# A fused forgetting-attention and gated feed-forward kernel on one core: the mask of its first blocks by TensorE, its first loads row by row, and a new order of the queues

## The chip, the cores and the metric

The kernel runs on one core of a Trainium2 chip. The core has five engines that take their own instruction queues in order and meet only at semaphores: TensorE (PE in the profile; its weight loads are PEld), VectorE (DVE), ScalarE (ACT), GpSimd (POOL) and SyncE (SP). SP, POOL and ACT also issue the DMAs, which 16 DMA engines carry out. The metric is device time in microseconds (us) of one execution; lower is better. Most executions of one kernel agree within a few tenths of a per cent, but the three runs shown below spread by 1.7%.

## The reference

```python
def _attn_ref(q, k, v, f):                    # q, k, v: (8, 8, 576, 64), f: (8, 8, 576)
    scores = scale * np.matmul(q, k.transpose(0, 1, 3, 2))
    cum = np.cumsum(np.log(np.clip(f, 0.0001, 1.0)), axis=-1)
    decay = cum[:, :, :, None] - cum[:, :, None, :]
    scores = np.where(causal, -1000000000.0, scores + decay)
    attn = np.exp(scores - np.max(scores, axis=-1, keepdims=True))
    attn = attn / (np.sum(attn, axis=-1, keepdims=True) + 1e-09)
    return np.matmul(attn, v)

def _moe_ref(x, w_gate, w_val, w_out, rms_g):  # x: (4608, 512), hidden width 1536
    xn = x / np.sqrt(np.mean(x * x, axis=-1, keepdims=True) + 1e-06) * rms_g
    g = xn @ w_gate
    return g * (1.0 / (1.0 + np.exp(-g))) * (xn @ w_val) @ w_out
```

Eight batches of eight heads attend causally over 576 positions with a decay by the cumulated log of the forget gate. The heads are then joined to rows of 512, normalised, and sent through a gated feed-forward. All arrays are float32 at the boundary; the kernel's matmuls take bfloat16.

## The kernel before, in words

**Tiles.** A block (b, qi) is 128 query positions of one batch, all eight heads; qi runs from 0 to 3, and qi = 4 (`LAST`) is the remaining 64 positions, which are taken for two batches together. The feed-forward works on groups of 512 rows: four blocks are one group (`home`). The first four batches run as a wave: group 0 is the block qi = 0 of batches 0 to 3, group 1 their qi = 1, and so on. Batches 4 to 7 then run one after the other, and group 8 collects all remainders.

**One block.** q, k are loaded with a cast to bfloat16 (POOL's DMA queue), and turned so that the head dimension lies on partitions: by PE for the first eight blocks (`turn_pe`, a transpose into the buffers `ff` and a copy to QT by DVE and to KT by ACT), by DMA for the others (`turn`, issued by SP). v is loaded in float32 and scaled by the decay factor (`scale_v`, tile Vs; POOL, but DVE for the very first). `score_block` multiplies KT with QT into one of two score buffers `sc`, ACT takes exp into PT, and the diagonal tile is masked: by POOL's affine_select (L596), for the four blocks of group 0 by a minimum with the tile `keep` on DVE (L602). `values` multiplies PT with Vs in two halves (even heads, odd heads), each into an `ff` buffer; an extra column of Vs gives the sum of weights, whose reciprocal scales the copy to x (L637, L639). `norm` forms the mean square (DVE, L667, or ACT, L653), takes its power of -1/2 on POOL (rs, L672), scales x to xn (L679, L683), turns it to xT by PE or DMA, and, for the first two groups, multiplies by rgT, the norm weights as four columns (L699).

**One group.** `gate` makes 12 pairs of products of xT with `wg` and `wv` (L771), tanh on ACT, two multiplications on DVE into hT (L786, L778). `project` multiplies hT with `wo` (L802) for each of four row tiles, ACT copies the result to `ores` (L814), and a DMA stores it (L820, or L828 for group 8). For the first two groups the gate products are cut into 256 rows, so that two blocks are enough to begin.

**First loads.** In wave order q and k of (b, 0), b = 0 to 3, come first, then the weights in four pieces each (`load_w`; c0 to c1 are 256, 256, 512 and 512 columns), then blocks (0, 1), (1, 1) and `wo`. The eight loads of (b, 0) fetch two neighbouring rows with one packet (`paired`), into tiles `T_two` that borrow the space of the rings `ores`, `ga` and `th`; `turn_pe` then needs 16 transposes of 64x64 and a copy with a stride. The four v loads of these blocks and rgT are issued by SP (`load_early`); rgT waits for the first Q copy.

**The order.** Nothing is scheduled by hand. Every piece of work is a `Unit` with an engine, a price in us, a due time (`key`), what it needs and which ring buffers it takes and gives back. `Plan.run` plays the units through in model time: a free engine takes the ready unit with the lowest key whose buffers are free, and the order in which units are taken becomes the order of the queues. The table `SHIFTS` moves the key of each unit, in the order in which the units were made, by so many hundredths. The prices and keys only set the order; the chip keeps to the order and the semaphores.

## Time and profile before

| | |
|---|---|
| three runs | 376.1, 378.63, 382.45 us (median 378.63) |
| the profiled execution | 376.78 us, its span 375.1 us, granted PE clock 0.997 |
| DMA traffic | 152922 packets, 45.05 MB; read from HBM 38.16 MB, written 9.44 MB |
| exp (L588) | 100 instructions of 1022 ns on ACT |
| gate products (L771) | 94.0 us with wg, 94.1 us with wv |
| projection (L802) | 102.2 us |
| scores (L569), values (L622) | 32.4 us, 36.9 us |

The span is the time from the first to the last instruction. The profile gives the busy time of each engine, 40 equal slices of it, the chain of work that ended last, and instructions grouped by line. In a timeline row stand start, length, engine, line, operation, what is written and what is read, and in brackets how long the engine had been idle before and what ended that. Matmuls are pipelined and their ends modelled, so a group's busy time is less than count times mean.

### The profile page before, as it was taken

The page shows a single profiled execution, that of the slowest core. Times are in us where ns is not written, and L with a number is a line of the kernel's source. Part 1 is how long each engine was busy: PE and PEld are TensorE (multiplying, and loading weights), DVE is VectorE, ACT ScalarE, POOL GpSimd, SP SyncE. Part 2 cuts the span into 40 slices and gives each one's busy share as a digit, 9 for nine tenths or more (in the row PEclk, how much of TensorE's full clock was granted, in tenths as well). Part 3 has the DMA queues.
Part 4 walks back from the last instruction along what each step waited for, and adds up shares of the span by engine and source line. Part 5 has one row for each costly group of instructions (what it writes and reads, how often), then busy time and mean ns, then how long its engine had stood idle before and what let it go on. Part 6 is the DMA issues. An engine that isn't in the chain of part 4 may idle for free.

```text
span 375.1 us, 8971 instructions
## 1 busy us (share of the span) xinstructions
PE 351.7 (94%) x3569; PEld 203.7 (54%) x3617; DVE 237.1 (63%) x460; ACT 206.7 (55%) x310; POOL 190.3 (51%) x259
## 2 busy tenths in 40 slices
PE   2669999999999998999999999999999999999995
PEld 2548876677755555545455455445455544444453
DVE  6758776599766857666545667655467782473520
ACT  5544666686677657735675667336777331333122
POOL 8776999999899738843534396424112000000000
PEclk9999999999999999999999999999999999999998
DMA  9999999999999959993958999960602000201024
GB/s 127 178 204 212 207 190 166 196 152 128 161 173 183 156 84 178 179 187 63 192 97 93 165 124 139 182 100 31 136 8 56 2 16 29 82 3 56 18 49 102
DMA packets 152922, 45.05 MB, mean 120 GB/s; under 512 B 141424, under 2 KB 147312, under 8 KB 152880
## 3 DMA queue, kind: packets, MB, share of 16 engines
q0 software_dynamic: 77856, 17.83, 53.9%
q1 hardware_dynamic: 74944, 26.58, 37.0%
q8 instruction: 28, 0.46, 0.5%
q14 instruction: 14, 0.11, 0.1%
q10 hardware_dynamic: 80, 0.07, 0.1%
HBM read 38.16 MB, written 9.44 MB: 127 GB/s over the span
## 4 chain that ended last, share of the span: by engine, by line
PE 85%; DVE 6%; DMA 5%; issue 2%; ACT 1%; POOL 1%; ACTq 0%; DVEq 0%; SPq 0%
PE ff L771 47%; PE ff L802 24%; PE sc L569 7%; PE ff L622 6%; DMA rgT<-in_moe_rms_g_dram 3%; DMA QT<-qk 2%; DVE junk L667 1%; DVE x L639 1%; DVE ga L786 1%; DVE hT L778 1%; DVE Vs L327 1%; DVE xn L683 1%; PE ff L692 0%; POOL rs L672 0%; PE ff L515 0%
## 5 line engine op out<-in xcount | busy, mean ns | idle before, releaser
L588 ACT ACTIVATE PT<-sc 128x1024 bf16<-128x1024 f32 x100 | 99.4, 1022 | 41.2 <-PE sc L569 35.5
L786 DVE SCALAR_TENSOR_TENSOR ga<-th,ff 128x512 f32<-128x512 f32 x108 | 73.6, 685 | 55.2 <-ACT th L784 51.1
L802 PE MATMUL ff<-wo,hT 128*128 128x512 bf16 (+1 forms) x421 | 102.2, 373 | 1.5 <-issue 0.5
L784 ACT ACTIVATE th<-ff 128x512 f32<-128x512 f32 x108 | 64.2, 598 | 64.5 <-PE ff L771 55.5
L771 PE MATMUL ff<-xT,wg 128*128 128x512 bf16 (+1 forms) x465 | 94.0, 340 | 2.5 <-DVE rden L637 0.9
L771 PE MATMUL ff<-xT,wv 128*128 128x512 bf16 (+1 forms) x472 | 94.1, 337 | 0.8 <-DVE hT L778 0.2
L778 DVE SCALAR_TENSOR_TENSOR hT<-ga,ff 128x512 bf16<-128x512 f32 x108 | 72.9, 685 | 26.9 <-PE ff L771 20.5
L771 PEld LDWEIGHTS <-wg 128*128 128x128 bf16 x528 | 50.2, 99 | 41.7 <-issue 2.2
L771 PEld LDWEIGHTS <-wv 128*128 128x128 bf16 x528 | 50.4, 98 | 40.3 <-issue 0.3
L802 PEld LDWEIGHTS <-hT 128*128 128x128 bf16 x444 | 40.5, 98 | 41.2
L596 POOL TENSOR_SCALAR_AFFINE_SELECT PT<-PT 128x1024 bf16<-128x1024 bf16 x32 | 36.2, 1134 | 41.9 <-ACT PT L588 38.7
L540 POOL TENSOR_TENSOR Vs<-v,decT 128x512 bf16<-128x512 f32 (+1 forms) x39 | 41.7, 1069 | 24.7 <-DMA v<-in_v_dram 24.1
L814 ACT COPY ores<-ff 128x512 f32<-128x512 f32 (+1 forms) x37 | 21.1, 572 | 39.5 <-PE ff L802 39.4
L622 PEld LDWEIGHTS <-PT 128*128 128x128 bf16 (+1 forms) x960 | 32.8, 103 | 17.4 <-issue 7.2
L622 PE MATMUL ff<-Vs,PT 128*128 128x65 bf16 (+1 forms) x960 | 36.9, 196 | 4.3 <-POOL Vs L541 3.0
L672 POOL TENSOR_TENSOR rs<-ms,mhalf 128x1 f32<-128x1 f32 (+1 forms) x28 | 17.9, 639 | 38.4 <-ACT junk L653 34.5
L569 PE MATMUL sc<-QT,KT 64*128 64x128 bf16 (+1 forms) x960 | 32.4, 211 | 3.7 <-DVE rgT L321 1.8
L569 PEld LDWEIGHTS <-KT 64*128 64x128 bf16 x960 | 24.0, 95 | 18.1 <-issue 14.3
L639 DVE TENSOR_TENSOR x<-ff,rden 128x256 f32<-128x256 f32 x72 | 30.6, 424 | 2.5
L398 POOL DMA_DIRECT2D qk<-in_q_dram x36 | 31.3, 873 | 0.6 <-issue 0.5
L398 POOL DMA_DIRECT2D qk<-in_k_dram x36 | 31.3, 872 | 0.3 <-DMA wo<-in_moe_w_out_dram 0.3
L683 DVE SCALAR_TENSOR_TENSOR xn<-x,rs,rgB 128x512 bf16<-128x512 f32 x28 | 24.4, 898 | 10.6 <-POOL rs L672 10.6
(67 smaller groups left out, 165.0 us busy)
## 6 DMA issues: line engine op xcount, KB each, us to landing
out_dram<-ores SPq DMA_DIRECT2D x32, 256.0 KB, 2.4
v<-in_v_dram SPq DMA_DIRECT2D x20, 256.0 KB, 5.4
qk<-in_k_dram POOLq DMA_DIRECT2D x28, 128.0 KB, 5.6
qk<-in_q_dram POOLq DMA_DIRECT2D x28, 128.0 KB, 6.2
v<-in_v_dram POOLq DMA_DIRECT2D x12, 256.0 KB, 6.9
wo<-in_moe_w_out_dram POOLq DMA_DIRECT2D x2, 768.0 KB, 11.4
wg<-in_moe_w_gate_dram POOLq DMA_DIRECT2D x2, 512.0 KB, 11.9
wv<-in_moe_w_val_dram POOLq DMA_DIRECT2D x2, 512.0 KB, 13.7
```

Source lines behind the costliest of these rows:

```text
L398: nc.gpsimd.dma_start(out=T_qk[h.slot][0:n, :].rearrange("p (h d) -> p h d", d=D), in_=src[b, :, p0:p0 + n, :].rearrange("h p d -> p h d"))
L540: eng.tensor_tensor(T_Vs[hv.slot][0:n, j, :, 0:D], T_v32[h.slot][0:n, :, :], bcast(dj, D), ALU.mult)
L569: nc.tensor.matmul(t[:, par, c:c + n], lhsT=kt[r, p, kj * 128:(kj + 1) * 128], rhs=qt[r, p, qi * 128:qi * 128 + n], start=True, stop=True)
L588: nc.scalar.activation(T_PT[hp.slot].rearrange("p (a c) -> p a c", a=2), T_sc[h.slot], ACT.Exp, scale=scale)
L596: nc.gpsimd.affine_select(out=d, in_=d, pattern=[[0, 1024 // n], [1, n]], compare_op=ALU.is_ge, fill=0.0, base=0, channel_multiplier=-1)
L622: nc.tensor.matmul(po[i * n:(i + 1) * n, p, :], lhsT=T_PT[h.slot][:, c:c + n], rhs=T_Vs[hold_Vs[x].slot][:, kj, 2 * p + par, :], start=(kj ...
L639: nc.vector.tensor_tensor(d, po[:, :, 0:D], bcast(rden[par], D), ALU.mult)
L771: nc.tensor.matmul(T_ff[h.slot][:, c:c + n], lhsT=w[:, dc, fc * 128:(fc + 1) * 128], rhs=xT[:, dc, t0:t0 + n], start=(dc == 0), stop=(dc = ...
L778: nc.vector.scalar_tensor_tensor(hT, in0=three[0], scalar=0.5, in1=three[1], op0=ALU.mult, op1=ALU.mult)
L784: th = act(0.6, key - 0.1, lambda: nc.scalar.activation(T_th[ht.slot], T_ff[hg.slot], ACT.Tanh, scale=0.5), [ug], take=[ht])
L786: a = dve(0.72, key - 0.1, lambda: nc.vector.scalar_tensor_tensor(T_ga[ha.slot], in0=T_th[ht.slot], scalar=1.0, in1=T_ff[hg.slot], op0=ALU ...
L802: nc.tensor.matmul(T_ff[hf.slot][:, 0:nc0], lhsT=T_hT[hold_hT[g].slot][:, fc, j * 128:(j + 1) * 128], rhs=wo[:, fc, cols], start=(fc == 0) ...
```

## The change

Seven things change in the code beside the table of the order.

1. *Mask.* For the four blocks of group 0, DVE's minimum goes. `keep` holds 0 on and above the diagonal and -1e30 below, and a new PE unit `bias` multiplies the identity with it into both halves of the score buffer, ahead of the scores; these then accumulate onto it (`start` is False) and exp makes zeros of the masked places. The unit has its own key, 0.6 before that of the scores.
2. *Loads.* `paired`, `T_two` and the ring `two` go; q and k of (b, 0) are loaded like all others, row by row into the ring `qk`, with four transposes of 128x128 and a plain copy.
3. *Values of the last 64* come as one PE unit that takes both `ff` buffers at once, not two units.
4. *The last product* (group 8, row tile 3) is cut into 384 and 128 columns instead of two times 256; the first piece is three units, the second one unit that waits for all of hT; the copy of the second piece is made by DVE. The products of group 8 end in the order of their row tiles (`ends`).
5. *Engines.* Vs of blocks (1, 0) and (2, 0) is scaled by DVE instead of POOL; the mean squares of blocks (0, 0) and (1, 0) are taken by ACT instead of DVE.
6. *Constants.* The fills of `mhalf` and of the extra column of x become a unit of their own on POOL.
7. *Prices* of many units, among them the loads, transposes and the model's factor for two moving queues.

The table SHIFTS is replaced as a whole; its entries were between -176 and 179 hundredths and are now between -1096 and 758. For the first queues its first row says, with the keys in the code, that POOL issues q before k of block (0, 0), and the mask tile after the first five of the eight loads.

```diff
-    -1, 1, 1, -1, 31, 0, -20, 14, -46, 25, -13, -12, -5, -46, 48, -19, 3, 10, 12, 42, -64, 71, 12, -62, 39, -70,
+    0, 0, 0, 0, -361, 0, -195, 96, 11, 156, -197, -432, -88, 210, -192, -173, 83, 80, -41, -101, -109, -86, 90, -63,
...
-        nc.gpsimd.memset(keep, 3.0e38)
-        nc.gpsimd.affine_select(out=keep, in_=keep, pattern=[[1, 128]], compare_op=ALU.is_ge, fill=0.0, base=0,
+        nc.gpsimd.memset(keep, 0.0)
+        nc.gpsimd.affine_select(out=keep, in_=keep, pattern=[[1, 128]], compare_op=ALU.is_ge, fill=-1.0e30, base=0,
...
-    iden_f = pool(0.95, -29.5, emit_ident)
-    keeps = pool(1.4, -28.5, emit_keep)
+    iden_f = pool(0.58, -29.5, emit_ident)
+    consts = pool(0.38, -28.45, emit_const)
+    keeps = pool(0.65, -28.5, emit_keep)
...
-            h = hold_qk[b, nm, j] = Hold("two" if paired(b, j) else "qk", 1)
-            if paired(b, j):
-                def emit(src=src, h=h):
-                    nc.gpsimd.dma_start(out=T_two[h.slot],
-                                        in_=src[b, :, 0:128, :].rearrange("h (p r) d -> p h r d", r=2))
...
+            h = hold_qk[b, nm, j] = Hold("qk", 1)
...
-        add, dur, eng = (dve, 0.8, nc.vector) if early else (pool, 1.5, nc.gpsimd)
+        add, dur, eng = (dve, 0.8, nc.vector) if early or (j == 0 and b in (1, 2, -1)) else (pool, 1.6 if j == 0 and b < WAVE else 1.25, nc.gpsimd)
...
                             nc.tensor.matmul(t[:, par, c:c + n], lhsT=kt[r, p, kj * 128:(kj + 1) * 128],
-                                             rhs=qt[r, p, qi * 128:qi * 128 + n], start=True, stop=True)
-        deps = pads if last_block[0] is None else [last_block[0]]
+                                             rhs=qt[r, p, qi * 128:qi * 128 + n], start=(b, qi) not in FAST,
+                                             stop=(b, qi) not in FAST or p == 3)
+        deps = list(pads) if last_block[0] is None else [last_block[0]]
         gives = []
+        if tiles[0][:2] in FAST:
+            h0 = holds[0]
+
+            def bias():
+                m = bass.AP(tensor=keep.tensor, offset=keep.offset, ap=[keep.ap[0], [0, 4], [1, 128]])
+                for par in range(2):
+                    nc.tensor.matmul(T_sc[h0.slot][:, par, :], lhsT=ident, rhs=m, start=True, stop=False)
+            u = pe(0.86, key - 0.6, bias, [iden, keeps] + ([last_bias[0]] if last_bias[0] else []), take=[h0])
+            last_bias[0] = u
+            deps.append(u)
...
-            if items[-1][1] == qi:
+            if items[-1][1] == qi and (b, qi) not in FAST:
...
-                if (b, qi) in FAST:
-                    def mk(hp=hp):
-                        d = T_PT[hp.slot].rearrange("p (h q) -> p h q", q=128)
-                        m = bass.AP(tensor=keep.tensor, offset=keep.offset, ap=[keep.ap[0], [0, 8], [1, 128]])
-                        nc.vector.tensor_tensor(d, d, m, ALU.min)
-                    masked[b, qi].append(dve(0.65, key, mk, [e, keeps]))
-                else:
-                    masked[b, qi].append(pool(1.1, key, mk, [e]))
+                masked[b, qi].append(pool(1.1, key, mk, [e]))
...
+        hpos = [Hold("ff", 1) for _ in range(2)]
+        units = []
+        for pars in ((0, 1),) if qi == LAST else ((0,), (1,)):
...
-        if b < WAVE and js[0] < LAST and len(js) == 1 and (js[0] or b in (0, 1)):
+        if b < WAVE and js[0] < LAST and len(js) == 1 and (js[0] or b in ()):
...
-            hf, cols = Hold("ff", 1), slice(x * nc0, (x + 1) * nc0)
+            hf, cols = Hold("ff", 1), slice(x * 384, 384 + x * 128) if halves == 2 else slice(0, DM)
+            wide = cols.stop - cols.start
+            parts = 3 - 2 * x
...
+            add, copy = (dve, nc.vector.tensor_copy) if x else (act, nc.scalar.copy)
...
+        if g == B:
+            ends.append(last)
```

More of the change, by code (lines that the diff above doesn't have):

```diff
@@ L578, in score_block @@
         cols = sum(len(items) * n / 128 for b, qi, items, n in tiles)
[L579 to L580 removed]
+        u = pe(0.19 + 0.25 * cols, key, emit, deps, take=holds, give=gives)
         last_block[0] = u
```

129 lines of the change are left out of this document (56 added, 73 removed), and 142 rows, old and new, of the table SHIFTS.

## The prediction

> **What bounds the kernel now.** I read the page first: its engine shares, its slices and the chain that ended last.
>
> ```profile
> span 375.1 us, 8971 instructions
> ...
> PE 351.7 (94%) x3569; PEld 203.7 (54%) x3617; DVE 237.1 (63%) x460; ACT 206.7 (55%) x310; POOL 190.3 (51%) x259
> ...
> PE   2669999999999998999999999999999999999995
> ...
> DMA  9999999999999959993958999960602000201024
> ...
> PE 85%; DVE 6%; DMA 5%; issue 2%; ACT 1%; POOL 1%; ACTq 0%; DVEq 0%; SPq 0%
> ```
>
> TensorE (PE) is busy for 351.7 of 375.1 us, and the chain that ended last lies on it for 85%. The slices say where the other 23.4 us are: PE shows 2 and 6 tenths in the first 19 us, 9 almost everywhere after that, and 5 in the last slice. The DMA row is at 9 for the first third of the span. So there are two questions: when does the dense PE work begin, and what holds the beginning up? The busy time by stage, cut where the first gate product starts and where the last product ends, gives the sizes:
>
> ```profile
> 0.00:24.07 24.07, 10.86 (x206) 9.19 (x207) 17.45 (x50) 12.95 (x17) 19.15 (x41) 1.00 1.29 163
> 24.07:370.85 346.78, 340.85 (x3364) 194.54 (x3411) 219.66 (x411) 193.21 (x293) 171.19 (x219) 1.00 0.90 117
> 370.85:375.10 4.25, 0.00 (x0) 0.00 (x0) 0.00 (x0) 0.59 (x1) 0.00 (x0) 0.77 0.30 93
> ```
>
> Columns: stretch and length, then PE, its weight loads, DVE, ACT and POOL busy. PE idles 24.07 - 10.86 = 13.21 us before the first gate product, 346.78 - 340.85 = 5.93 us in the stream, and 4.25 us at the end. Three terms follow: start, stream, tail. The chain of waits, in order of time, and the timeline of the start come next:
>
> ```profile
> 9.16 12.37 DMA rgT<-in_moe_rms_g_dram
> ...
> 24.07 3.57 PE ff L771 x16
> ...
> 30.28 4.37 PE ff L771 x40
> ```
>
> ```profile
> 9.16 3.89 SPq L453 DMA_DIRECT2D rgT<-in_moe_rms_g_dram  x1
> ...
> 9.65 0.69 DVE L602 TENSOR_TENSOR PT<-PT,keep 128x1024 bf16<-128x1024 bf16 x1
> ...
> 12.36 1.02 ACT L588 ACTIVATE PT<-sc 128x1024 bf16<-128x1024 f32 x1 [2.03 <-PE sc L569]
> ...
> 14.06 0.68 DVE L602 TENSOR_TENSOR PT<-PT,keep 128x1024 bf16<-128x1024 bf16 x1
> ...
> 15.97 0.40 PE L622 MATMUL ff<-Vs,PT 128*128 128x65 bf16 x4
> ...
> 17.05 0.73 DVE L522 COPY QT<-ff 128x512 bf16<-128x512 bf16 x1
> ...
> 18.48 0.42 DVE L639 TENSOR_TENSOR x<-ff,rden 128x256 f32<-128x256 f32 x1
> ...
> 20.16 1.04 POOL L540 TENSOR_TENSOR Vs<-v,decT 128x512 bf16<-128x512 f32 x1 [1.96 <-DMA v<-in_v_dram]
> ...
> 21.30 0.56 POOL L672 TENSOR_TENSOR rs<-ms,mhalf 128x1 f32<-128x1 f32 x1
> ...
> 21.56 0.69 DVE L699 TENSOR_TENSOR xT<-ff,rgT 128x512 bf16<-128x512 bf16 x1 [1.32 <-DMA rgT<-in_moe_rms_g_dram]
> ...
> 23.32 0.69 DVE L699 TENSOR_TENSOR xT<-ff,rgT 128x512 bf16<-128x512 bf16 x1
> ```
>
> The first gate product needs both xT tiles of blocks 0 and 1, and two things hold them. The norm weights rgT are issued at 9.16 and land 12.37 us later, at 21.5; the first xT (L699) waits for them. The second xT, at 23.32, hangs on rs at 21.30, which stood on POOL behind the Vs of 20.16, which waited 1.96 us for a v load. Block 1's own chain was long too: exp ended at 13.38, DVE masked only at 14.06, the values product ran at 15.97. The start is thus set by loads, and by DVE and POOL taking their work in order. Two rows of the chain also give a price for cold PE: 16 products of 256 columns in 3.57 us (223 ns each) at 24.07, but 40 in 4.37 us (109 ns) at 30.28.
>
> **The change part by part.** All is set against this execution's own 376.78 us (span 375.1 and 1.7 around it).
>
> *Mask on PE.* Four DVE masks (L602, 0.68 to 0.69 us each) go; eight matmuls of 128x512 come, two for a block. No row has a cold 512-column matmul; from the 223 ns above it is 2 x 223 = 446 ns, so 0.89 us a block and 3.6 us in all. I cost them at nothing, because PE idles 13.21 us there and the unit has only to wait for the mask tile, the identity and a free score buffer. If that cover is gone (the score buffer still read by exp, or the mask tile late on POOL behind the first loads), PE's queue stands still, the transposes and values behind it too, and 0.89 us each for the two blocks of the first gate is 1.8 us on the path.
>
> *Less on DVE and POOL.* The Vs scaling of blocks 1 and 2 goes from POOL (1.04 us each) to DVE, and the sums of squares of blocks 0 and 1 from DVE to ACT:
>
> ```profile
> L653 ACT ACTIVATE junk<-x 128x513 bf16<-128x513 f32 x2 | 1.3, 628 | 0.8 <-DVE x L639 0.8
> ...
> L667 DVE SCALAR_TENSOR_TENSOR junk<-x 128x513 bf16<-128x513 f32 x2 | 1.4, 698 | 0.1
> ```
>
> Plain instead of strided PSUM copies shorten the four Q copies, as line 524 stands to 522:
>
> ```profile
> L522 DVE COPY QT<-ff 128x512 bf16<-128x512 bf16 x4 | 2.9, 720 | 0.0
> ...
> L524 DVE COPY QT<-ff 128x512 bf16<-128x512 bf16 x4 | 1.7, 421 | 0.4 <-PE ff L515 0.4
> ```
>
> DVE loses 4 x 0.68 + 2 x 0.70 + 4 x 0.30 = 5.3 us and gains two Vs of about 0.69 (the duration of its 512-column rows in the timeline): net 3.9 us of the 17.45 it works before 24.07. For block 1: exp to values falls from 2.59 us (13.38 to 15.97) to about 0.2, saving 2.4; of the Q copy and the next mask that stood before x at 18.48 about 1.0 goes; and rs no longer stands behind the Vs that waits, saving some 1.6 (x done at 18.90, its squares about 0.8 later, rs at 21.30). Alone that brings the second xT 5.0 us forward, to about 18.3. Then rgT is what is late next: two xT of 0.69 us after 21.54 end at 22.9, so the first gate comes at 23.0 if rgT does not move, a gain of 1.1.
>
> *One-row loads.* Eight q and k loads come as 1024 packets instead of 512: 4096 more packets on POOL's queue, and 16 transposes become 4 on an idle PE (nothing). The rate of the two kinds stands in the DMA rows of 3:5 us (two-row packets alone) and of 34:35 us (nearly all one-row packets):
>
> ```profile
> DMA packets 1040, 0.26 MB, mean 129 GB/s; under 512 B 1040, under 2 KB 1040, under 8 KB 1040
> ```
>
> ```profile
> DMA packets 1088, 0.20 MB, mean 200 GB/s; under 512 B 1072, under 2 KB 1072, under 8 KB 1088
> q0 software_dynamic: 1088, 0.20, 228.5%
> ```
>
> 1040 in 2 us is 0.98 us a load of 512; 1072 in 1 us is 0.96 us a load of 1024. Alone, then, the one-row load costs nothing more. If each small packet took the time of a two-row one, a load would take 1.97 us and eight of them 7.9 us more. Bounds: 0 and 7.9. I take 2.0, near the lower end, since the second row has the very packets in question, but not 0, because the early loads share the engines with v. In the Trainium skill, "DMA: Bandwidth & Descriptors" (Why small descriptors are slow) gives a fixed overhead of about 3 cycles a packet beside one cycle for 32 B. By an estimate from that page two packets of 128 B need 14 cycles where one of 256 B needs 11, so 8 x 0.98 x 0.27 = 2.1 us more; the 34:35 row shows no such surplus, and the sum would be the same by it to 0.1 us.
>
> The gate's first weights are behind these packets:
>
> ```profile
> 9.03 1.55 POOL L421 DMA_DIRECT2D wg<-in_moe_w_gate_dram  x2
> ```
>
> ```profile
> wg<-in_moe_w_gate_dram POOLq DMA_DIRECT2D x1, 256.0 KB, 10.5
> ```
>
> They land at 9.03 + 10.5 = 19.5 now and at about 21.5 then. But rgT stands in the other queue, behind the v packets. In 14:18 us the two queues moved packet for packet:
>
> ```profile
> q0 software_dynamic: 982, 0.47, 86.8%
> q1 hardware_dynamic: 977, 0.25, 46.9%
> ```
>
> There a software packet took 0.868 x 64 / 982 us, 57 ns; in 34:35 it is 2.285 x 16 / 1088 us, 34 ns. Opposite one-row packets the 7.5 us that rgT still needs after 14 could shrink towards 34/57 of that, 3 us at most and by my estimate 2; if the start is bound by the number of packets, it comes no sooner than now. The first gate starts then between 21.6 (first weights) and 23.0 (rgT unmoved). I take the middle, 22.3: **start -1.8 us**, bounds -3.5 and +3.4 (weights 7.9 us later, gate at 27.5).
>
> *What is late next.* The following weights and the loads of the next four blocks are 2 us later while PE is 1.8 earlier. From 24 to 54 us PE has hardly any room:
>
> ```profile
> 24.00:54.00 30.00, 29.20 (x315) 24.48 (x316) 22.85 (x48) 17.65 (x30) 25.23 (x32) 1.00 1.54 205
> ```
>
> Only 0.80 us of idle; the four products of the first output group are ready as filler once wo has come. I give back **+0.8 us**, bounds 0 and 3.8 (both shifts in full).
>
> *The order.* The new table of shifts changes the queues of all engines for the whole stream, PE, SP's transposes and POOL's issues among them. The trace cannot show it; what it shows is that 5.93 us of idle are there to win, in pieces no longer than this one:
>
> ```profile
> PE ff L771 <- DVE rden L637: 0.9, 1, 0.9
> ```
>
> Many small waits can be neither all removed nor much improved by one order: I take **-0.5 us**, bounds -4 (two thirds of the idle gone) and +6 (idle doubled). The last-64 values in one piece have the same matmuls; only the first evacuation waits for the second half, hidden while two of four ff buffers are free; without that cover four times about 0.4 us (half of one). Split constants, new prices and the plain buffers change no work.
>
> *The tail.* The last product is cut into 384 and 128 columns instead of twice 256, the same column count, and its last copy is 128 wide, on DVE, then stored by SP and ACT. Before, another row tile ended the kernel:
>
> ```profile
> 371.09 0.59 ACT L814 COPY ores<-ff 128x512 f32<-128x512 f32 x1 [0.70 <-PE ff L802]
> 371.70 0.34 SPq L820 DMA_DIRECT2D out_dram<-ores  x1
> ```
>
> ```profile
> out_dram<-ores SPq DMA_DIRECT2D x1, 256.0 KB, 2.0
> out_dram<-ores SPq DMA_DIRECT2D x3, 64.0 KB, 1.9
> out_dram<-ores ACTq DMA_DIRECT2D x1, 64.0 KB, 2.2
> ```
>
> A copy of 512 columns took 0.59 us. For 128 I take 0.3 (the Q copies' 0.42 is above it): -0.3. The store of 64 rows lands in 1.9 to 2.2 us against 2.0: +0.1. **Tail -0.2 us**, bounds -0.6 and +0.3.
>
> **Sum:** 376.78 - 1.8 + 0.8 - 0.5 - 0.2 = 374.3; the three runs before have a median of 378.63, 1.85 above the profiled one, with a lowest of 376.1. I add 0.7 of this spread, as the new runs will scatter likewise: 375.0.
>
> **The rivals.**
> *A. The loads take over (slower).* Place: POOL's DMA queue from 2 to 30 us. If each one-row packet costs what a two-row one costs, the first weights land at 27.4, the gate starts at 27.5, 3.4 us late, and the next four blocks, 7.9 us late, add another 2 when PE runs out of filler: 376.8 + 5.4 = 382. With s us more for the loads the gate starts at 19.6 + s and the give-back is 0.4 s (0.8 for 2.0); with order and tail at -0.7 the sum s - 4.5 + 0.4 s - 0.7 turns positive at s = 3.7, which is where it decides. For it: the DMA row at 9 and rgT already 12.37 us in flight. Against it: the 1088 packets of 34:35.
> *B. Nothing arrives.* rgT stays at 21.5, the gate starts at 23.0, and the 1.1 us go in the stream before 54 us, where DMA sets the pace: 376.8 - 1.1 + 1.1 - 0.2, with the same 0.7 about 377.3. For it: the 0.80 us of idle there.
> *C. Everything arrives.* rgT early, gate at 21.0 to 21.6, -2.8; the order takes 3 us of the 5.93; tail -0.5: 376.8 - 6.3 = 370.5. For it: block 1 has 5 us to gain and idle that the waits show as avoidable. Against: loads at 9 tenths.
> *D. The mask units block PE's queue* as priced above, +1.8: the start gains nothing, and 376.8 + 0.8 - 0.5 - 0.2 with the 0.7 is 377.6, close to B and counted with it.
>
> **How the numbers follow.** The forecast of 374 to 376.5 has 0.48, C 0.18, B with D 0.22, A 0.12. The predicted time is 375.0. The range goes from C's 370.5 to 381, which leaves out most of A and the better part of what lies under C: about 2 in 10. Two per cent, 7.6 us, is about what a measurement of this kernel can tell from no change. Faster by that means below 371.1, about half of C: 0.10. Slower means above 386.2, beyond A's 382 and reached only with a worse order on top: 0.04. The rest, 0.86, is within.
>
> **What would show it.** Right: no DVE mask in the first 24 us and 128x512 matmuls before the scores; values of block 1 before 14 us; rs of block 1 not behind a waiting Vs; first gate product at 21.6 to 23.0; PE idle in the stream of 5 to 7 us; 4 us from the last product to the end. Wrong: the first gate after 24.1 with the first weights landing late (A); a PE wait before the masks' matmuls (D); idle between 30 and 60 us above 2 us (B); stream idle below 3 us (C) or above 9 (order). The forecast falls if rgT lands after 22, or if the stream's idle is far from 6.

## The result and the profile after

The changed kernel took 382.65 us (median of 12 runs, 379.74 to 389.29), the kernel before 377.75 us beside it (12 runs, 375.57 to 382.45). The ratio is 1.0133, 95% interval 1.0088 to 1.0177: 1.3% longer, clear of the scatter though under two per cent, where 375.0 us (370.5 to 381.0) had been forecast. Ratios leave out runs more than 1.5% above the fastest of the same kernel. The profiled execution took 379.88 us, 3.1 us more than the 376.78 us of the one before. The page of the changed kernel, the rows that answer to those shown of before, with the row of the granted PE clock (first that of before, then that of after):

```profile
span 378.1 us, 8861 instructions
...
PE 357.2 (94%) x3529; PEld 202.3 (53%) x3529; DVE 232.2 (61%) x457; ACT 207.4 (55%) x313; POOL 189.7 (50%) x255
...
PE   3979999999999998899999999999999999999995
...
PE 66%; POOL 14%; DMA 8%; issue 4%; DVE 4%; ACT 2%; SPq 1%; DVEq 0%; POOLq 0%
```

```profile
PEclk9999999999999999999999999999999999999998
```

```profile
PEclk9969999999999999999999999999999999999999
```

PE is as busy as before (94%), and the slices look alike. What differs is the chain that ended last: PE held 85% of it, now 66%, and POOL 14%, DMA 8%; and the clock, which is at 6 tenths in the third slice (18.9 to 28.4 us). The stages, cut again at the first gate product and the last product (columns as above):

```profile
0.00:22.97 22.97, 12.97 (x113) 7.72 (x114) 13.81 (x45) 13.27 (x20) 18.07 (x37) 0.98 1.41 153
22.97:373.56 350.59, 344.27 (x3420) 194.57 (x3417) 218.13 (x411) 194.16 (x294) 171.65 (x219) 0.99 0.91 117
373.56:378.10 4.54, 0.00 (x0) 0.00 (x0) 0.29 (x1) 0.00 (x0) 0.00 (x0) 0.86 0.42 116
```

The start is 1.10 us shorter (22.97 against 24.07), the tail 0.29 us longer (4.54 against 4.25), the stream 3.81 us longer (350.59 against 346.78): together the 3.0 us by which the span grew. The timeline of the start:

```profile
8.90 1.06 PE L571 MATMUL sc<-keep,ident 128*128 128x512 bf16 x2
...
14.58 0.43 PE L617 MATMUL ff<-Vs,PT 128*128 128x65 bf16 x4
...
18.80 1.05 POOL L531 TENSOR_TENSOR Vs<-v,decT 128x512 bf16<-128x512 f32 x1 [2.48 <-DMA v<-in_v_dram]
...
19.94 0.55 POOL L668 TENSOR_TENSOR rs<-ms,mhalf 128x1 f32<-128x1 f32 x1
20.17 0.69 DVE L695 TENSOR_TENSOR xT<-ff,rgT 128x512 bf16<-128x512 bf16 x1 [3.14 <-DMA rgT<-in_moe_rms_g_dram]
...
22.21 0.68 DVE L695 TENSOR_TENSOR xT<-ff,rgT 128x512 bf16<-128x512 bf16 x1
...
22.97 1.26 PE L767 MATMUL ff<-xT,wg 128*128 128x256 bf16 x5
```

The mask's product is made first, and nothing masks on DVE. Block 1's values run at 14.58 us instead of 15.97. rgT lands 1.4 us earlier, the first xT being released at 20.17 instead of 21.56. But the second xT comes only at 22.21: rs of block 1 stands at 19.94, right behind a Vs on POOL that waited 2.48 us for its v load. It is the Vs of block 3, which the change left on POOL.

Then the lead is lost, most of it within seven microseconds. The stretch in which the changed kernel's granted clock is at half (stretch and length, PE's busy time and count, granted clock, DMA share, GB/s):

```profile
21.87:28.69 6.82, 6.03 (x38) 0.50 1.28 205
```

The page of before shows no such stretch, but the first clock entry of its trace comes only at 28.44 us, and its products ran as slowly until then: 16 of them in 3.57 us, as the prediction's chain shows. So both kernels begin the gate at half rate and reach full rate at about the same time. The gate products that follow the first 32, before and after:

```profile
30.12 1.04 PE L771 MATMUL ff<-xT,wg 128*128 128x256 bf16 x8
```

```profile
29.81 1.91 PE L767 MATMUL ff<-xT,wv 128*128 128x256 bf16 x16
```

Of the 1.10 us, 0.31 are left. Gate products done after 44 us (timeline windows of that line alone; PE's busy time and count, then weight loads, clock, DMA share, GB/s), before first, after second:

```profile
0.00:44.00 44.00, 18.19 (x136) 13.90 (x136) 1.00 1.36 184
```

```profile
0.00:44.00 44.00, 18.60 (x136) 14.11 (x136) 0.92 1.42 178
```

Both kernels have done 136. The rest goes mainly at one place. PE waits 4.1 us for xT in the changed kernel, 3.43 of them at once. The stretch around it, first before, then after:

```profile
138.58 0.08 DVE L667 DVE_READ_ACCUMULATOR junk<-x 128x1 f32 x1
...
139.63 0.54 POOL L672 TENSOR_TENSOR rs<-ms,mhalf 128x1 f32<-128x1 f32 x1
...
140.21 0.75 DVE L683 SCALAR_TENSOR_TENSOR xn<-x,rs,rgB 128x512 bf16<-128x512 f32 x1 [0.95 <-POOL rs L672]
...
141.03 1.23 SPq L703 DMA_TRANSPOSE xT<-xn  x1
...
142.98 4.07 SPq L411 DMA_DIRECT2D v<-in_v_dram  x3
...
145.63 1.67 PE L771 MATMUL ff<-xT,wg 128*128 128x512 bf16 x7 [0.89 <-DVE rden L637]
```

```profile
141.17 0.97 POOL L400 DMA_DIRECT2D qk<-in_k_dram  x1
...
141.69 0.07 DVE L663 DVE_READ_ACCUMULATOR junk<-x 128x1 f32 x1
...
142.16 0.57 POOL L668 TENSOR_TENSOR rs<-ms,mhalf 128x1 f32<-128x1 f32 x1
...
142.68 1.80 POOL L400 DMA_DIRECT2D qk<-in_q_dram  x2
...
142.96 1.31 SPq L413 DMA_DIRECT2D v<-in_v_dram  x2
143.07 0.74 DVE L679 SCALAR_TENSOR_TENSOR xn<-x,rs,rgB 128x512 bf16<-128x512 f32 x1
...
144.36 3.04 SPq L699 DMA_TRANSPOSE xT<-xn  x1
...
144.46 0.90 POOL L400 DMA_DIRECT2D qk<-in_k_dram  x1
...
153.14 1.04 PE L767 MATMUL ff<-xT,wg 128*128 128x512 bf16 x4 [3.43 <-DMA xT<-xn]
```

The last xT transpose of group 3, that of block (3,3), went out at 141.03 us before, ahead of three v loads; PE used it at 145.63. After, xn comes at 143.07: its mean square is done at 141.76 instead of 138.66, and rs then stands behind a POOL load until 142.16. Two v loads go ahead on SP, and POOL has issued four q and k loads by 145.4. In the chain of waits the transpose then flies 8.73 us:

```profile
144.36 8.73 DMA xT<-xn
```

PE has nothing else to do and stands for 3.43 us, where it had waited 0.89 us at this place before.

To compare kernels whose orders differ, the table below uses lost time: the time passed, less what PE's products up to then would take at full rate. It is worked out from PE's weight loads in each trace, with 0.1085 us for a gate or value product of 256 columns, 0.216 for one of 512 or of the output, 0.034 for a score, 0.030 or 0.019 for the last product of attention, and nothing for transposes and mask. The names are those of the experiments below.

```
at us  before  after    a0    a1    e2    e4    e5    e6  e_all e_row e_norow
   24    21.7   21.3  21.4  22.2  21.2  21.3  21.7  21.3   22.2  22.1   22.0
   50    26.8   26.8  26.8  26.8  26.8  26.8  26.8  26.8   27.3  27.5   27.4
   90    31.1   30.4  30.8  32.2  30.4  30.6  31.1  30.0   31.5  32.1   31.8
  100    31.8   31.0  34.4  33.1  32.1  32.1  32.2  32.0   32.0  32.7   32.2
  140    30.4   30.3  33.4  31.4  30.1  31.3  30.6  30.2   30.6  32.2   30.8
  160    32.0   34.2  39.2  38.4  36.8  33.2  32.8  32.7   35.0  37.0   32.3
  190    32.5   35.7  42.7  41.6  38.8  36.1  35.1  35.6   35.9  37.9   33.3
  240    32.2   35.1  42.7  41.7  39.1  35.6  34.6  35.0   35.7  37.7   33.0
  340    32.0   34.7  42.1  41.4  38.7  35.2  34.1  34.6   35.4  37.6   32.8
```

Whatever the start was, at 50 us every kernel of the table in the new order stands at 26.8, as the kernel before does (e1, which is not in it, at 27.2 by the same working). Then they part again: at 90 and 100 us the changed kernel of the first profile is 0.7 and 0.8 us ahead, at 140 us it is level. Between 140 and 160 it loses 2.3 us more than the kernel before, up to 190 another 1.0, and later nothing.

The table also holds what no list of waits shows. Some traces have stretches of 3.41 us at a granted clock of 0.50 behind a long wait; by an estimate from these two figures each takes 1.7 us from a PE that is busy all through it, so that such a wait costs more than its length.

### The profile page after: what moved, and what is told of

The parts are those of the page before. It is cut to its first block, busy times and chain, and to the rows that moved or that the text cites. A ratio compares the mean times of both kernels' runs of the same rounds, so it can differ in the third digit from the quotient of the medians.

```text
span 378.1 us, 8861 instructions
## 1 busy us (share of the span) xinstructions
PE 357.2 (94%) x3529; PEld 202.3 (53%) x3529; DVE 232.2 (61%) x457; ACT 207.4 (55%) x313; POOL 189.7 (50%) x255
## 4 chain that ended last, share of the span: by engine, by line
PE 66%; POOL 14%; DMA 8%; issue 4%; DVE 4%; ACT 2%; SPq 1%; DVEq 0%; POOLq 0%
PE ff L767 39%; PE ff L801 19%; POOL qk L400 5%; DMA v<-in_v_dram 4%; PE ff L617 4%; PE sc L560 4%; DMA xT<-xn 3%; POOL Vs L531 3%; POOL v L413 2%; POOL PT L597 1%; POOL rs L668 1%; ACT PT L589 1%; POOL Vs L532 1%; SPq L451 1%; DVE xn L679 1%
## 5 line engine op out<-in xcount | busy, mean ns | idle before, releaser
L801 PE MATMUL ff<-wo,hT 128*128 128x512 bf16 (+2 forms) x444 | 102.6, 373 | 0.0
L767 PE MATMUL ff<-xT,wg 128*128 128x512 bf16 (+1 forms) x480 | 95.7, 342 | 4.2 <-DMA xT<-xn 4.1
L767 PE MATMUL ff<-xT,wv 128*128 128x512 bf16 (+1 forms) x480 | 96.1, 339 | 1.0 <-DVE ga L782 0.9
L774 DVE SCALAR_TENSOR_TENSOR hT<-ga,ff 128x512 bf16<-128x512 f32 x108 | 72.1, 683 | 15.7 <-PE ff L767 13.4
L531 POOL TENSOR_TENSOR Vs<-v,decT 128x512 bf16<-128x512 f32 (+1 forms) x37 | 39.4, 1066 | 20.8 <-DMA v<-in_v_dram 19.9
L400 POOL DMA_DIRECT2D qk<-in_q_dram x40 | 34.9, 874 | 2.1 <-PE ff L767 1.1
L400 POOL DMA_DIRECT2D qk<-in_k_dram x40 | 34.8, 873 | 0.3 <-PE ff L767 0.3
L633 DVE RECIPROCAL rden<-ff 128x4 f32<-128x4 f32 x72 | 13.0, 180 | 33.0 <-PE ff L617 32.6
```

The costliest lines, as they stand in the source:

```text
L400: nc.gpsimd.dma_start(out=T_qk[h.slot][0:n, :].rearrange("p (h d) -> p h d", d=D), in_=src[b, :, p0:p0 + n, :].rearrange("h p d -> p h d"))
L531: eng.tensor_tensor(T_Vs[hv.slot][0:n, j, :, 0:D], T_v32[h.slot][0:n, :, :], bcast(dj, D), ALU.mult)
L767: nc.tensor.matmul(T_ff[h.slot][:, c:c + n], lhsT=w[:, dc, fc * 128:(fc + 1) * 128], rhs=xT[:, dc, t0:t0 + n], start=(dc == 0), stop=(dc = ...
L774: nc.vector.scalar_tensor_tensor(hT, in0=three[0], scalar=0.5, in1=three[1], op0=ALU.mult, op1=ALU.mult)
L801: nc.tensor.matmul(T_ff[hf.slot][:, 0:wide], lhsT=T_hT[hold_hT[g].slot][:, fc, j * 128:(j + 1) * 128], rhs=wo[:, fc, cols], start=(fc == 0 ...
```

## The experiments

Two theories stood against each other. One: the edits cost time (one-row loads above all). The other: the new order does. Two kernels answer it; the rest look for the place. In the kernels named e1 to e6 the line numbers are three or four higher than in the changed kernel. `behind(a, b, ...)` takes issue units out of the finished order and puts them right behind `a`; `named[...]` is the unit that issues that transfer, `P.units[n]` the nth unit.

**a0 and a1: the changed kernel, unaltered, twice more.**

> The changed kernel once more, unaltered, as the yardstick beside the others. In its first profile PE waited 3.4 us at 149.7 us for the last xT tile of group 3, whose DMA transpose took 8.7 us from issue to landing behind two v loads. Theory (order): the new order was planned with DMA prices below what the chip takes, so its slack is thin and stalls of this kind stand in every execution; then this wait of 2 to 5 us is there again at the same place and the time is 1.0 to 1.5% above the kernel before. Rival (scatter): the stall was bad luck of one execution; then it is below 1 us here, and the loss must lie elsewhere.

> The changed kernel unaltered, once more, beside e6 on the same chip. Two measurements of it gave 1.0133 and 1.0215. By theory 1 it stands 1.0 to 2.0% above e6; by theory 2 within 0.7% of it.

a0: 386.93 us (median of six, one of which took 2036.68 us; without it 386.67), ratio 1.0215 (1.0156 to 1.0274), with 7.2 us of PE waits for xT, the longest 4.6. a1: 385.68 us against 378.2. Its ratio is given as 1.0056 (0.9991 to 1.0121), but it rests on three of the twelve runs; by the medians of all runs it is 1.020. Against e6 the medians put a1 1.3% higher (theory 1), the two ratios 0.3% lower (theory 2), so that comparison stays open. In the profiled execution of a1, 386.55 us, PE waits for xT at two places, 4.4 us at 155 and 1.7 at 189, as it does in a0 at 157 and 190; the first of them, and the clock rows of a0 and a1:

```profile
155.28 1.46 PE L767 MATMUL ff<-xT,wg 128*128 128x512 bf16 x3 [4.43 <-DMA xT<-xn]
```

```profile
PEclk9969999998999999899999999999999999999998
```

```profile
PEclk9969999999999999699999999999999999999999
```

The clock falls to half for 3.41 us at 92.81 and at 157.66 in a0, behind waits of 2.0 and 4.6 us, and for 6.83 us at 154.23 in a1, around the wait of 4.4 us; behind the 3.43 us of the first profile it does not. With it the table adds up: in a0 2.0 us of wait and 1.7 at half rate stand against 3.6 us lost between 90 and 100; in a1 4.4 us of wait and, from 155.28 on, 2.4 at half rate against 7.0 lost between 140 and 160. This third measurement of the same program also starts its gate products later, at 25.10 instead of 22.97, and still stands at 26.8 at 50 us. The changed kernel's time thus varies by how long two or three waits come out and by whether the clock falls behind them: 377.7 to 388.9 us in a1's runs, while the kernel before had 375.4 to 384.1 beside it.

**e_all: the edits in the order of before.** The mask on PE, the one-row loads, Vs of (1,0) and (2,0) on DVE, squares of (0,0) and (1,0) on ACT and the short last product, each put in by what a unit emits, with the table and the prices of before. The core of it:

```diff
+        if j == 0 and b in (1, 2):
+            eng = nc.vector
...
-    T_two = [t[0:64, :].bitcast(BF16).rearrange("p (h r d) -> p h r d", r=2, d=D) for t in T_ores + T_ga + T_th]
+    T_two = [t.bitcast(BF16)[:, 0:H * D] for t in T_ores + T_ga + T_th]
...
+            line.insert(at, Unit("PE", 0, 0, bias, 0))
```

> The kernel before, with its own table of shifts, prices and so its own order of all queues, but with the edits of the work put in: mask by PE (bias units put ahead of the scores, the DVE minimum left out), one-row loads in the same buffers, Vs of blocks (1,0) and (2,0) on DVE, mean squares of (0,0) and (1,0) on ACT, last product as 384 and 128 columns with its last copy on DVE. Left as before: the last-64 values in two pieces, the split constants, the order of the first queues. Theory (order): the edits are worth what the start showed, 0.5 to 2 us, and the loss is the order's; time 375.5 to 377.5, that is 0.2 to 0.6% below the kernel before, first gate product at 22 to 24 us and no new wait above 1 us after 60 us. Rival (edits cost): the 4096 more packets or the mask on PE make the kernel slower; then it is 1% or more above the kernel before in this order, too.

379.07 us, ratio 1.005 (1.002 to 1.008). These edits thus cost about half a per cent, and the order the larger part of what a0 lost beside it. What e_all leaves out (the last-64 values as one unit, the constants as a unit of their own, the order `ends`) is counted with the order here; no run tries it alone. **e_row** and **e_norow** split the edits: the loads alone, and all but the loads.

> The kernel before, in its own order, with one edit: q and k of the first four blocks come row by row (4096 packets more), with four transposes of 128x128 and a plain copy. Theory a (the one-row loads are what the edits cost): as e_all, ratio 1.004 to 1.008, first gate product 0.5 us or more later than in the kernel before. Theory b (they cost nothing on the path, as the 34:35 row of the kernel before has it): 0.998 to 1.002, and the first gate product within 0.3 us of 24.07.

> The kernel before, in its own order, with the mask on PE, Vs of (1,0) and (2,0) on DVE, squares of (0,0) and (1,0) on ACT, and the short last product, without the one-row loads. Theory a (the loads cost and the other edits gain): first gate product at 22.5 to 23.3, ratio 0.994 to 0.999. Theory b (the early part is bound by loads in either form, and the other edits give nothing on the whole): 0.999 to 1.005, the first gate product at 23.5 or later.

e_row: 1.0039 (1.001 to 1.0068), first gate product at 25.05 us. e_norow: 1.0023 (0.9985 to 1.0061), first gate product at 24.82. Neither theory is borne out alone. In e_row PE waits for the later one-row loads, and block 1's values stand behind those waits in its queue:

```profile
16.61 0.61 PE L508 MATMUL ff<-ident,th 128*128 128x128 bf16 x4 [1.15 <-DMA th<-in_k_dram]
...
17.69 0.40 PE L612 MATMUL ff<-Vs,PT 128*128 128x65 bf16 x4
```

They come at 17.69 us, where before they came at 15.97. The k load of that ring tile was 8.2 us in flight instead of 6.9. In e_norow no load is longer, but the mask's product of a later block waits for exp to give its score buffer back, with the transposes and block 1's values behind it:

```profile
14.46 1.01 PE L589 MATMUL sc<-keep,ident 128*128 128x512 bf16 x2 [0.79 <-ACT PT L597]
...
17.83 0.40 PE L628 MATMUL ff<-Vs,PT 128*128 128x65 bf16 x4
```

So in the order of before the edits give nothing at the start; they need an order that puts block 1's values ahead, which the new one does. In e_all and e_row a second loss comes at 147 to 149 us, where the last xT of group 3 lands 5.3 us after its issue at 141.72 and 143.60 (lost time 30.6 to 35.0 and 32.2 to 37.0 between 140 and 160). The same transposes decide there, though the loads ahead of them are in the old order: PE waits 2.1 and 2.3 us for them, and the clock falls to half for 3.41 us behind both waits. So the room at this place is thin in the order of before, too, and part of what the edits cost is lost there.

**e1 and e1b: one of two queues moved.** Behind the transpose of block (3,3) go only the v loads (e1, first line) or only the q and k loads (e1b, second line).

```diff
+        behind(named["xT", 3, 3], named["v", 5, 0], named["v", 5, 1])
...
+        behind(named["xT", 3, 3], named["k", 5, 1], named["k", 5, 0], named["q", 5, 1], named["q", 5, 0])
```

> The changed kernel with two instructions moved: on SP the v loads of blocks (5,0) and (5,1) are issued just behind the last xT transpose of group 3 instead of just ahead of it; nothing else is altered. Theory (v ahead): the 2048 packets of these loads stand in the same hardware queue ahead of the transpose; then its time to landing falls from 8.7 to about 4 us, the 3.4 us wait of PE goes nearly whole (below 0.7), and the kernel is 2.5 to 3.5 us faster than the changed one. Rival (POOL loads): the DMA engines are simply full of the four q and k loads of blocks (5,0) and (5,1); then landing stays above 6 us and less than 1.5 us is won.

> The changed kernel with the four q and k loads of blocks (5,0) and (5,1) issued on POOL just behind the issue of the same xT transpose in the emitted order, v loads left ahead of it. POOL runs on by itself, so they come only a little later, by what stands between. Theory (v ahead): the transpose still stands behind 2048 v packets, at most the sharing gets thinner; landing 6 us or more, PE's wait above 1.5 us. Rival (POOL loads): landing falls to about 4 us and the wait goes.

e1: 384.07 us, 1.0169 (1.0128 to 1.021). e1b: 384.61 us, 1.0163 (1.0109 to 1.0216). Either lies a little below a0, within the intervals. In the profiled execution of e1, at 390.39 us the slowest of its six, the transpose flew 7.0 us (the longest of the view of that tile, 136 to 160 us):

```profile
DMA to landing us min/median/max: 5.9/6.5/7.0
```

That is 1.8 to 2.4 us less than the 8.7 and 9.4 us of the unaltered kernel, and not the 4 us of the theory: beside the q and k loads alone it still flies above 6 us, as the rival had it. The wait for xT at 155 us falls to 1.4 us, but PE then waits 2.7 us for a mask of POOL at 159 and 3.3 us for the next group's xT at 192. In e1b it waits 4.1 us as before: the edit moves the loads only in the emitted order, and POOL does not wait for SP, so its loads still went out at 143.70 to 147.3 us, and the transpose flew as long as before:

```profile
146.93 8.62 DMA xT<-xn
```

**e2 and e3: both queues moved.** e2 has the first two lines, e3 all four.

```diff
+        behind(named["xT", 3, 3], named["v", 5, 0], named["v", 5, 1])
+        behind(P.units[427], P.units[420], named["k", 5, 1], named["q", 5, 0], named["q", 5, 1], named["k", 5, 0])
...
+        behind(named["xT", 4, 3], named["v", 5, 4])
+        behind(P.units[618], P.units[440], named["q", 6, 0], named["q", 5, 4], named["k", 5, 4])
```

> The changed kernel with its own order, but for one spot: on SP the transpose of xT of block (3,3) goes ahead of the two v loads of (5,1) and (5,0), and on POOL the four q and k loads of (5,0) and (5,1) go behind the next Vs scaling, the first K transpose of (5,0) with them. In the profile of the unaltered changed kernel this transpose took 9.4 us from issue to landing, behind six loads, and PE waited 4.6 us for it at 152 us. Theory 1 (single late transposes in stretches full of loads): the transpose lands within 5 us, PE waits under 1 us for it, and the ratio to the kernel before falls from 1.0215 to about 1.010 (4 to 5 us less, about 382). Theory 2 (the new order has no room anywhere, so that a stall removed comes back at the next place): that wait goes too, but the next ones (the transpose of block (4,3) at about 185 us, masks, q and k turns) grow by as much, and the ratio stays at 1.015 to 1.022. Theory 3 (the flight time is not made by these loads): the flight stays at 7 to 9 us.

> As e2, and the second spot treated in the same way: the transpose of xT of block (4,3) goes ahead of the v load of (5,4), and the q and k loads of (5,4) and the q load of (6,0) go behind the next PT mask on POOL. In the unaltered changed kernel it took 6.2 us and PE waited 2.6 us for it at 188 us. Theory 1: both waits are under 1 us, and the time is 2 to 3 us below that of e2, within 0.5% of the kernel before or up to 0.5% above it. Theory 2: no lower than e2 by more than 1 us; the lost time shows at other places.

e2: 384.08 us, 1.0163 (1.0108 to 1.0219). e3: 386.74 us, 1.0173 (1.0109 to 1.0237). The times are theory 2's, but the trace shows why. The flights of the xT transposes issued between 136 and 160 us (the view of that tile), in a0:

```profile
DMA to landing us min/median/max: 5.7/7.5/9.4
```

in e2:

```profile
DMA to landing us min/median/max: 3.1/3.6/4.0
```

and the timeline of e2, with what PE waited for instead:

```profile
150.34 0.97 POOL L401 DMA_DIRECT2D qk<-in_k_dram  x1
...
153.94 1.13 POOL L600 TENSOR_SCALAR_AFFINE_SELECT PT<-PT 128x1024 bf16<-128x1024 bf16 x1
...
155.12 0.52 PE L620 MATMUL ff<-Vs,PT 128*128 128x65 bf16 x7 [4.69 <-POOL PT L600]
```

The flight fell from 9.4 to 4.0 us at most, and the wait for it is gone. But the loads now stood on POOL ahead of a mask that PE needs: POOL issued them from 150.34 to 153.94, then masked, and PE waited 4.69 us. One stall was exchanged for another by the edit itself. In e3 PE waits 3.89 us for the same mask at 157.54; the wait for the transpose of block (4,3) is gone, and 1.78 us for ga come at 193.02.

**e4: the mask ahead of the loads.**

```diff
-        behind(P.units[427], P.units[420], named["k", 5, 1], named["q", 5, 0], named["q", 5, 1], named["k", 5, 0])
+        behind(P.units[594], P.units[427], P.units[423], P.units[420],
+               named["k", 5, 1], named["q", 5, 0], named["q", 5, 1], named["k", 5, 0])
```

> As e2, but on POOL the mask of PT that stood behind the moved loads goes ahead of them: the four q and k loads of (5,0) and (5,1) and the first K and Q transposes of block 5 go behind that mask, and the Vs scaling of block 5 that waits for its v load goes behind the loads. In e2 the transpose of block (3,3) landed within 4.0 us and the wait for it was gone, but PE waited 4.7 us at 155 us for that mask. Theory 1 (the loss at 150 us is one deadline, met when neither the transpose nor the mask stands behind loads): no wait of PE above 1 us between 145 and 165 us, lost time between 140 and 160 us under 3 us (6.7 in e2, 5.8 in the unaltered changed kernel), and a ratio of 1.005 to 1.012. Theory 2 (something else is late there next): again 4 us lost between 140 and 165 us, by another wait, ratio 1.015 to 1.022.

380.83 us (378.3 to 383.15), ratio 1.0086 (1.0056 to 1.0117). Lost time between 140 and 160 us falls from 5.8 in a0 to 1.9, as theory 1 had it, and the clock does not fall there; the condition named there, "no wait of PE above 1 us", fails by one wait of 1.9 us for ga at 160 us.

**e5: POOL's scalings away from xn.** At 88 us a0 lost 3.6 us in another way (2.0 us of wait, and the clock at half behind it). e5 is e4 with two Vs scalings of POOL behind its next two loads there.

```diff
+        behind(P.units[155], P.units[377], P.units[372])
```

> As e4, and at 88 us two Vs scalings on POOL (which in the unaltered changed kernel ran right behind an rs, while DVE's xn stood at 3.19 us instead of 0.75 us and the ga behind it made PE wait 2.0 us) go behind POOL's next v and q loads. Theory 1 (xn is slow because POOL works beside it): xn at 88 to 92 us takes 0.75 to 1.0 us, PE waits under 0.5 us for ga there, and the time is 1 to 2 us below that of e4. Theory 2 (xn is slow for another reason, or ga is late by its own chain): xn stays above 1.4 us or the wait for ga stays at 1 us or more, and the time is as in e4.

The timeline of a0, with DVE's xn between two scalings of POOL and PE's wait for ga:

```profile
88.59 1.03 POOL L531 TENSOR_TENSOR Vs<-v,decT 64x512 bf16<-64x512 f32 x1
88.65 3.19 DVE L679 SCALAR_TENSOR_TENSOR xn<-x,rs,rgB 128x512 bf16<-128x512 f32 x1 [0.45 <-POOL rs L668]
...
90.25 1.03 POOL L531 TENSOR_TENSOR Vs<-v,decT 128x512 bf16<-128x512 f32 x1
...
92.48 1.58 PE L767 MATMUL ff<-xT,wv 128*128 128x256 bf16 x8 [2.04 <-DVE ga L782]
```

and that of e5:

```profile
88.83 0.75 DVE L682 SCALAR_TENSOR_TENSOR xn<-x,rs,rgB 128x512 bf16<-128x512 f32 x1 [0.46 <-POOL rs L671]
...
89.28 0.73 POOL L415 DMA_DIRECT2D v<-in_v_dram  x1
```

xn takes 0.75 us in e5, where POOL ends an rs and issues a load beside it, and 3.19 us in a0, while POOL scales twice. But that is no gain of the edit. e4, which has the scalings where a0 has them, shows

```profile
89.87 0.74 DVE L682 SCALAR_TENSOR_TENSOR xn<-x,rs,rgB 128x512 bf16<-128x512 f32 x1
```

since xn came there only behind the first scaling; in the first profile it took 0.74 us, in a1 1.74 us, all in one order. Whether xn and the scalings meet varies from run to run. e5: 379.72 us, ratio 1.0064 (1.0037 to 1.0091), 1.1 us below e4 by the medians; the intervals of the two overlap, so that e5 is not shown to win anything over e4.

**e6: rs ahead of a scaling.**

```diff
+        behind(max(P.units[914], P.units[915], P.units[1191], key=line.index), P.units[422], P.units[221], P.units[223], P.units[916])
```

> As e5, and on POOL one more step in the same stretch: the rs of the blocks of group 4 and the two loads behind it go ahead of the second Vs scaling of block 5. In e5 this rs ran at 156.8 us, behind two Vs scalings and two loads, xn at 157.6 us and ga at 158.9 us followed, and PE waited 1.9 us for ga at 159.7 us. Theory 1: this wait falls under 0.5 us, lost time at 200 us is about 33 us (34.2 in e5, 32.3 in the kernel before), and with the shorter tail the time comes within 0.4% of the kernel before: ratio 1.000 to 1.005. Theory 2 (what is left comes from elsewhere, or a new wait takes its place): ratio 1.005 to 1.010, as e5.

380.55 us, ratio 1.0083 (1.0042 to 1.0123): theory 2. The wait for ga is gone, but PE waits 2.04 us for a mask of POOL at 160.47 and 1.25 us for xT at 182.95. The pieces moved by hand in e6 win nothing. No version beat the kernel before: the best, e_norow, e_row and e5, are within 0.7% of it.

## Why the prediction was wrong

**The order is the step that failed.** The prediction has "Many small waits can be neither all removed nor much improved by one order: I take -0.5 us, bounds -4 (two thirds of the idle gone) and +6 (idle doubled)". With the give-back that makes +0.3 us for the stream; it grew by 3.81 us in the profiled execution. PE's wait for one transpose of xT, 3.43 us where the kernel before had waited 0.89 at that place, makes 2.5 us of it. By the ratios the order, with the edits that e_all leaves out, costs from 0.8% (1.0133 in the result against 1.005 for e_all) to 1.6% (a0's 1.0215), 3 to 6 us: up to the upper bound; by a1's ratio of three runs it would cost next to nothing.

The argument looked at the idle that was there to win and not at what the old order kept away: a transpose that must be there within 5 us, in a stretch in which both queues are full. The trace of before held the clue: its own last transpose was used 4.6 us after its issue. A new order that issues such a piece 3 us later, behind and beside six loads, has no room; e4 got 1.3% back of a0's 2.15% by moving these units and the mask beside them alone (0.5% against the first measurement, 1.0133, where the intervals overlap). That is shown for the place at 150 us; for the one at 88 us it is not, since e4, without the edit of e5, loses 1.5 us between 90 and 100, where e5 loses 1.1 and a0 3.6. That the order is tight because it was searched under lower prices of the loads is only argued: no run here searched another.

The idle was misread, too. Of the 5.93 us, 2.5 are 46 gaps of 0.04 to 0.08 us, most of them where two products start 0.43 us apart instead of 0.216, in a trace with 48 fewer matmuls than weight loads (3569 and 3617): they look like missing records, not like idle time. So about 3.5 us were there to win. After the change no record is missing, and PE idles 350.59 - 344.27 = 6.32 us. The sign "PE idle in the stream of 5 to 7 us" was met although the mechanism had failed.

**The clock was left out.** The prediction priced cold PE from the chain, but had no term for how long PE stays at half rate. It does so to about 28.5 us in both kernels, for 5.7 us of the stream after and 4.4 us before, and again behind long waits.

**Start, -1.8 (bounds -3.5 to +3.4).** Right in kind, smaller in size: -1.10, with the gate at 22.97 inside 21.6 to 23.0. rgT was indeed late next for the first xT. The statement that rs of block 1 "no longer stands behind the Vs that waits" was wrong: the change moved the scalings of blocks 1 and 2, and rs stood behind that of block 3. In the other kernels with the new order the gate started at 22.67 to 25.49.

**Give-back, +0.8 (0 to 3.8).** The size came out by luck. By 30 us 0.79 of the 1.10 us had gone, but not by late loads: PE idles 0.48 us between 30 and 50 us before and 0.26 after. An earlier start at half rate wins half as much, and full rate came no sooner (28.69 us against 28.44). Rival B let the whole gain go before 54 us because DMA sets the pace; the gain went, but no run shows that DMA took it.

**One-row loads, +2.0 of DMA.** About right: in e_row block 1's values came 1.7 us later and the k load among the last flew 1.3 us longer; the whole is +0.4%. In the changed kernel the first piece of wg, issued at 10.82 and 10.2 us in flight, landed at 21.0, against 21.5 forecast and 19.5 before. Rival A, where they take the start over by 3.4 us, did not happen.

**Mask on PE at nothing.** Held in the new order, with 1.06 us for the two matmuls of a block instead of 0.89: no PE wait before the mask's products but 0.5 us for the mask tile. In the order of before it cost a place in PE's queue (e_norow), rival D's mechanism.

**Tail, -0.2 (-0.6 to +0.3).** It went the other way: +0.29. The last copy was 0.29 us as taken, and it ends 0.38 us behind the last product (373.94 and 373.56) instead of 0.83 (371.68 and 370.85). But three stores then stand one behind the other on SP, and the kernel ends 4.16 us behind the last copy instead of 3.42; the prediction had 0.1 us for the stores:

```profile
373.47 1.99 SPq L832 DMA_DIRECT2D out_dram<-ores  x3
373.65 0.29 DVE L815 COPY ores<-ff 128x128 f32<-128x128 f32 x1 [15.65 <-PE ff L801]
```

**The sum.** The terms as written, 376.78 - 1.8 + 0.8 - 0.5 - 0.2, make 375.1 and not 374.3: the give-back was left out. With the 0.7 for the scatter the forecast would have been 375.8.

**The scatter.** 0.7 us were added for it. The runs of the changed kernel lie 2.8 us above its profiled one in the median. Waits of 2 to 5 us come and go from run to run, and the clock falls behind some of them: the median granted clock of the twelve runs is 0.9845, that of the profiled one 0.989, which by an estimate from these two is 0.0045 x 380 = 1.7 us, one stretch of 3.41 us at half rate. The chance of 0.04 to 0.12 for the slow side was too low: the order's own upper bound of +6 takes the sum to 382.3, beyond the range, and should have had a rival of its own.

## What to carry to other kernels

When a change replaces the whole order of a tuned kernel, do not price the order by the idle that is left: list the transfers that PE uses within a few us of their issue, and count what the new queues put ahead of each. Read the row of the granted clock beside the waits: an earlier start at half rate wins less than it shows, and a long wait can cost half rate behind it. When one unit is moved out of a queue's way, see at once what stands behind the place where it is put.

## What the runs showed of the hardware

After 60 us the traces have 14 waits of PE of 2.0 us or more. Behind or around 11 of them (2.0 to 4.7 us) the granted clock is 0.50 for 3.41 or 6.83 us, beginning within 1.2 us of the wait's end; behind three (3.43 us in the changed kernel, 2.62 in a0, 2.04 in e6) it stays full. No other stretch at half clock stands between 60 us and the last product. The kernel before, with no wait above 0.9 us, has none. Why three waits were spared is open.

DVE's xn (two large inputs from SBUF) takes 0.75 us in most of its 28 instances in a kernel: in 308 of 392 over all traces it is under 0.8 us. Of the 84 longer ones 80 have an elementwise instruction of POOL beside them, most at 1.4 to 1.9 us, one in e3 at 3.17 us and one in a0 at 3.19 us, through a scaling, a cast, an rs and a second scaling in a row; but four of 1.42 to 1.58 us have only POOL's loads beside them (one in the kernel before, at 76.82), and 39 of the short ones stand beside POOL's elementwise work, too. The Trainium skill, "SBUF — State Buffer" (SBUF: two separate sides), says that DVE with two SBUF inputs and POOL share a pair of ports under a lock that the first holds for its whole instruction; the traces agree with it but for those four, and in a0 DVE did not get it between POOL's instructions either, for 2.4 us.

An SBUF transpose by DMA of 128x512 flew 2.7 to 4.2 us at 136 to 160 us in e2 and e4, with the loads moved away from it, 7.0 us in e1 beside four one-row loads of the other queue, and 8.6 to 9.4 us behind two v loads with those four beside it.
